# GFNet mixing and hard-swish MLP on one core: the filter step of batches two to eight with real and imaginary part side by side in columns

## The chip, the cores and the metric

The kernel runs on one core of a Trainium2 chip. The metric is the device time of one execution in microseconds (us). One execution was also recorded by the hardware profiler; its page and its trace are what is read here. Engines are named as the profile names them: PE (TensorE, the matmuls), PEld (its weight loads), DVE (VectorE), ACT (ScalarE), POOL (GpSimd), SP (SyncE, which issues most DMAs).

## The reference

Two blocks in a row, all in float32. The first is a global filter: a real Fourier transform over the sequence, a product with a complex filter per frequency and channel, and the inverse transform. The second is an MLP with hard-swish on every token.

```python
batch, seq, dim = (8, 3008, 256)          # n_freq = 1505
X = np.fft.rfft(x, axis=1)
Y = X * (filt_r + 1j * filt_i)[None, :, :]
y = np.fft.irfft(Y, n=seq, axis=1)

h = y.reshape(24064, 256) @ w_in          # d_ff = 2048
g = h * np.clip(h + 3.0, 0.0, 6.0) / 6.0
out = g @ w_out
```

## The kernel before

The transform of length 3008 = 47 x 64 is done in two stages of matmuls with tables of cosines and sines, and the way back likewise. Per batch (numbered 0 to 7 in the code, one to eight here) the stages are: `a_unit` or `a6_unit` (sums over 47, results stored to `z_tmp` in HBM), `t2_load` (reads them back with k, part and column over the partitions), `b_unit` (sums over 64: the spectrum of two rows of k, in a PSUM bank), `f_unit` (products with the filter), `y_unit` (their sums: the filtered spectrum `y`), `bi3_unit` (first stage of the way back for three `y`, copied to a tile `t3`), `g3_store` (to `g_tmp` in HBM), `t4_load` and `n_five` or `n_unit` (second stage, giving `xn`, the token columns of the MLP). k runs over 24 values, four to a filter table, so a batch has six tables and twelve `f_unit`s.

The MLP works on 47 blocks of 512 tokens, each in 8 steps of 256 hidden columns. A step multiplies with Strassen-like sums: `up_1` to `up_5` make seven products with `w_in` in the PSUM tiles `al` and `be`, `hswish`, `g_sums` and `g_last` form the operands on DVE, `down` makes seven products with `w_out` in the four `po` banks. All matmuls go through `strips` (line 768), two column halves of 64 at a time. A step without other work takes 6.1 us.

The spectral stages of the next batch are put into these steps by hand: `at(step, fn, ...)` places a function at a step, `places(n)` holds the steps of `f_unit`, `y_unit` and `bi3_unit`, and the loop at the end writes the instruction streams in that order. Every engine works its stream in order. For batches three to eight (`n` 2 to 7), with k the first step of the batch's own tokens, `a6_unit` of the last chunk is at step k-41, `t2_load` and `table_load` of tables 0 and 1 at the end of step k-40, the first `b_unit` and `f_unit` in step k-38. In that step DVE runs `g_sums`, then `f_unit`, then `up_2b` (line 797, h from `be`) and the sum of `up_3` (line 802, h from `al`). TensorE's last `up` product, `up_5`, writes into `al` again, so it comes after line 802.

Real and imaginary part lie on the two halves of the partitions. `b_unit` (line 539) fills a bank with the real part on partitions 0 to 63 and the imaginary part on 64 to 127, two k in the columns. `f_unit` multiplies the whole bank with the filter (line 559), and for the crossed products each half with the other half of the filter (lines 563, 564). `y_unit` subtracts or adds halves (lines 573, 574), on 64 partitions each.

`table_load` (lines 259, 261) puts the filter in a table of 128 partitions: frequencies k + 47 q on the even rows of a quarter and the mirrored ones on the odd rows, hence a partition stride of two. For batches two to eight it issues 8 DMAs of 64 KB on SP's queue; there are two buffers (`FB = 2`), so table c waits for the last `f_unit` of table c-2. SP also issues `x_load`, `t2_load`, `t4_load` and all stores of the result, in program order.

Of the kernel before, what the change touches and what calls it, by code (L numbers as in the profile page):

```python
# [10 lines left out]
FP32 = mybir.dt.float32  # L11
I32 = mybir.dt.int32
AXT = mybir.ActivationFunctionType
# [14 lines left out]
NA = 47  # L28
# [50 lines left out]
def _make_tables():  # L79
# [12 lines left out]
    for k in range(KH):  # L92
        at = k // 4 * 4 + (0, 2, 1, 3)[k % 4]
        for j in range(HC):
            tw = 2 * np.pi * (((np.arange(2 * NA) * HC + j) * k) % N) / N
            to = 1 + j * ATOM + at % 2 * KH + at // 2
            w0[X0:X0 + 2 * NA, to], w0[X0:X0 + 2 * NA, to + NU] = np.cos(tw), -np.sin(tw)
    wi = np.zeros((P, 3, NC))
    wf = np.zeros((P, 4, 64))
    at_of = [q % 2 * 32 + q // 2 * 2 if q < 32 else (31 - q) % 2 * 32 + (q - 32) // 2 * 2 + 1 for q in range(64)]  # L100
    for q in range(64):
        g, sign = (q, 1.0) if q < 32 else (31 - q, -1.0)
        co, si = (f([2 * np.pi * ((j * g) % NC) / NC for j in range(HC + 1)]) for f in (np.cos, np.sin))
        ab = np.concatenate([co, np.zeros(HC - 1) if q == 63 else si[1:HC]])
        cd, dc = ab * np.where(np.arange(NC) > HC, -1.0, 1.0), np.roll(ab, HC)
        at = at_of[q]
        wi[at, 0], wi[HALF + at, 0] = cd, sign * dc
        cs, sn = (np.array([f(2 * np.pi * ((j * g) % NC) / NC) for j in range(HC)]) for f in (np.cos, np.sin))
        if g % 32 == 0:
            sn = np.zeros(HC)  # L110
        for r in range(0, P, HALF):
            wf[r:r + 32, g % 2, at % 32], wf[r + 32:r + 64, g % 2, at % 32] = cs, sn
            wf[r:r + 32, g % 2, 32 + at % 32], wf[r + 32:r + 64, g % 2, 32 + at % 32] = -sign * sn, sign * cs

        for h in range(2):
            s = -1.0 if h and g % 2 else 1.0
            wf[h:HALF:2, 2, at], wf[HALF + h::2, 2, at] = s * cs, s * sn
            wf[h:HALF:2, 3, at], wf[HALF + h::2, 3, at] = -s * sign * sn, s * sign * cs
        wi[at, 1], wi[HALF + at, 1] = cd, -cd
        wi[at, 2], wi[HALF + at, 2] = sign * dc, sign * dc  # L120
    start = np.eye(P)
# [45 lines left out]
                    direct[HALF + at_of[q], k - KH + TC, n * TOK:(n + 1) * TOK] = -2 / N * first_of(np.sin(th), n)  # L167
    wai = np.concatenate([t.reshape(P, -1) for t in (groups, ones, first, last)], axis=1)
    f = np.float32
    return wa.astype(f), w0.astype(f), wai.astype(f), wi.astype(f), wf.astype(f), start.astype(f), direct.astype(f)  # L170


@with_exitstack
def kernel(
# [8 lines left out]
):  # L183
    nc = tc.nc

    wa_np, w0_np, wai_np, wi_np, wf_np, start_np, direct_np = _make_tables()
    wa_d = nc.inline_tensor(wa_np, name="wa_t").ap()
    w0_d = nc.inline_tensor(w0_np, name="w0_t").ap()
    wai_d = nc.inline_tensor(wai_np, name="wai_t").ap()
    wi_d = nc.inline_tensor(wi_np, name="wi_t").ap()  # L190
    wf_d = nc.inline_tensor(wf_np, name="wf_t").ap()
    start_d = nc.inline_tensor(start_np, name="start_t").ap()
    direct_d = nc.inline_tensor(direct_np, name="direct_t").ap()
# [32 lines left out]
    edge = wai[:, ds(2 * (NJ + 1) * NA, ND)]  # L226
    edges = edge.rearrange("p (j n) -> p j n", n=TOK)
    wi = const.tile([P, 3, NC], FP32, name="wi")
    xs = const.tile([P, 3, XC, D], FP32, name="xs")
    ft_all = const.tile([P, FB * TC, D], FP32, name="ft")  # L230
    ft = [ft_all[:, ts(i, TC), :] for i in range(FB)]
# [10 lines left out]
    def raw(src, row, ap):  # L242
        return bass.AP(tensor=src.tensor, offset=src.offset + row * D, ap=ap)


    def table_load(b, c):
        n = TC if b else 2 * TC
        if n == TC:
            t = ft[(b * NT + c) % FB]
            st["ft", b, c] = t  # L250
        else:
            t = x0_at(HC * D - TC * D * c, 2 * TC * D).rearrange("p (k d) -> p k d", k=n) if c else ft_all
            for i in range(2):
                st["ft", b, c + i] = t[:, ts(i, TC), :]
        for src, p0 in ((filt_r, 0), (filt_i, HALF)):
            q = nc.gpsimd if p0 and b == 0 and c else nc.sync
            for r in range(2):
                o = p0 + 32 * r
                q.dma_start(t[o:o + 32:2, :, :].rearrange("p k d -> p (k d)"),
                                  raw(src, c * TC + NA * r, [[2 * NA * D, 16], [1, n * D]]))  # L260
                q.dma_start(t[o + 1:o + 32:2, :, :],
                                  raw(src, NA * (2 - r) - c * TC, [[2 * NA * D, 16], [-D, n], [1, D]]))
# [125 lines left out]
    def x0_at(o, n):  # L388
        return w_all.rearrange("p a b c m -> p (a b c m)")[:, ds(NP * 14 * P - HC * D + o, n)]
# [141 lines left out]
    def b_unit(b, i):  # L531
        c, r = divmod(2 * i, TC)
        if b != 1:
            t = st.pop(("t2", b, c))
            ps = [bank(b) for k in range(2)]
            for s_ in range(2):
                for ri in range(2):
                    for k in range(2):
                        nc.tensor.matmul(ps[k][ds(ri * 64 + s_ * 32, 32)].rearrange("p (v d) -> p v d", v=2),  # L539
                                         wf[ts(k, 64), s_, ts(ri, 32)], t[ts(k, 64), :, s_, :], start=True, stop=True)  # L540
            for k in range(2):
                st["ps", b, i + k] = ps[k].rearrange("p (u d) -> p u d", u=2)
            return
        ps = bank(b).rearrange("p (u d) -> p u d", u=2)
        for u in range(2):

            strips(ps[:, u, :], wf[:, 2:4, :].rearrange("p a m -> p (a m)"), st["t2", b, c][:, r // 2 + 2 * u, :], start=True, stop=True)
        st["ps", b, i] = ps

    def f_unit(b, i):  # L550
        c, r = divmod(2 * i, TC)
        ps = st.pop(("ps", b, i))
        f = st["ft", b, c][:, r:r + 2, :]

        pool_, n1, n2 = (hp, "h0", "h1") if b == 0 and i & 2 else (sp, "s1", "s2")
        s1, s2 = (pool_.tile([P, 512], FP32, name=n).rearrange("p (u d) -> p u d", u=2) for n in (n1, n2))

        re, im = slice(0, HALF), slice(HALF, P)
        nc.vector.tensor_tensor(out=s1, in0=ps, in1=f, op=ALU.mult)
        if ("tf", b, c) in st:  # L560
            nc.vector.tensor_tensor(out=s2, in0=ps, in1=st["tf", b, c][:, r:r + 2, :], op=ALU.mult)
        else:
            nc.vector.tensor_tensor(out=s2[re], in0=ps[re], in1=f[im], op=ALU.mult)
            nc.vector.tensor_tensor(out=s2[im], in0=ps[im], in1=f[re], op=ALU.mult)
        st["y", b, i] = s1, s2

    def y_unit(b, i):
        s1, s2 = st["y", b, i]
        if b == 0 and i % 2 == 0:
            st["y0"] = t1p.tile([P, 2, 2, D], FP32, name="t1")  # L570
        y = yp.tile([P, 2, D], FP32, name="y") if b else st["y0"][:, i % 2, :, :]
        re, im = slice(0, HALF), slice(HALF, P)
        nc.vector.tensor_tensor(out=y[re], in0=s1[re], in1=s1[im], op=ALU.subtract)
        nc.vector.tensor_tensor(out=y[im], in0=s2[re], in1=s2[im], op=ALU.add)
        st["y", b, i] = y
# [15 lines left out]
    def bi3_unit(b, i):  # L591
        ys = [st.pop(("y", b, i + v)) for v in range(3)]
        c = psU.tile([P, 512], FP32, name="be")
        banks = [psF.tile([P, 512], FP32, name="psf", tag="f") for ri in range(2)]
        t = t3p.tile([P, 3, 2, D], FP32, name="t3")
        to = [t[:, q, :, :].rearrange("p u d -> p (u d)") for q in range(3)]
        for r in range(3):
            for v in range(2):
                for ri in range(2):
                    x, u, ps, o = (2, v, c, ri) if r == 2 * ri else (v, r - 1 + ri, banks[ri], r - 1 + ri)  # L600
                    nc.tensor.matmul(ps[ts(v, 64), ts(o, D)], wi[ts(ri, 64), 0, :], ys[x][ts(ri, 64), u, :], start=True, stop=True)  # L601
            if r == 0:
                nc.vector.tensor_copy(out=to[2][:, 0:2], in_=c[:, 0:2])
        nc.scalar.activation(out=to[1], in_=banks[1], func=AXT.Copy)
        st["t3", b, i] = t
        st["bi3"] = to[0], banks[0], to[2], c

    def bi3_copies():
        if "bi3" in st:
# [3 lines left out]

    def g3_store(b, i):
        t = st.pop(("t3", b, i))
        for v in range(2):
            nc.gpsimd.dma_start(g_d[b, :, :, ds(2 * (i + v), 2), :].rearrange("c ri u d -> c ri (u d)"),
                                t[ts(v, 64), 0:2].rearrange("p ri u d -> p ri (u d)"))
        for u in range(2):
            nc.gpsimd.dma_start(g_d[b, :, :, 2 * (i + 2) + u, :], t[ts(u, 64), 2])  # L620

    def g0_first(i):
        t = st["t3", 0, i]
# [142 lines left out]
    def strips(ps, w, x, **kw):  # L766
        for o in range(0, P, STRIP):
            nc.tensor.matmul(ps[ds(o, STRIP)], w[:, ds(o, STRIP)], x, skip_group_check=True, **kw)  # L768
# [214 lines left out]
    with tc.manual_schedule():  # L983
# [111 lines left out]
        def wai_load():  # L1095
            nc.sync.dma_start(wa[:, 528:], wa_d[:, 528:])
            nc.sync.dma_start(wai, wai_d[:, 0:NW])


        half = 0  # L1100
# [222 lines left out]
```

## Time and profile before

| | |
|---|---|
| median of 3 runs | 2602.68 us (2601.38 to 2606.01) |
| the profiled execution | 2602.51 us |
| its span in the profile | 2600.7 us |
| granted TensorE clock | 1.0 |
| DMA queue of SP (q1) | 114141 packets, 148.25 MB |
| filter loads of batches two to eight | 336 DMAs of 64 KB |

The page gives busy time and its share of the span for each engine, the chain of work that ended last, and groups of equal instructions: line, engine, operation, tiles written and read, shapes, count, then busy time, mean duration of one in ns, and the engine's idle time before them with what ended it. The timeline gives start (us from the span's start), duration, engine, line, operation and count, and in brackets the idle time before. A float32 matmul appears as two records, one for each pass.

### The profile page before, as it was taken

What the parts mean: (1) busy time and instruction counts of PE and PEld (TensorE: products, weight loads), DVE (VectorE), ACT (ScalarE), POOL (GpSimd) and SP (SyncE); (2) the same over time, 40 slices, a digit from 0 to 9 for tenths busy, and PEclk for the clock granted to TensorE, in tenths of its full rate; (3) what the DMA queues carried; (4) which work ended last, traced back from release to release, by engine and by line L of the source; (5) the groups of instructions that cost most, each with busy time, mean ns of one, the idle gap of its engine ahead of it and who ended that gap; (6) DMA issues with size and microseconds to landing.
All of it is one profiled execution on the core that took longest, in us unless ns stands there. A gap on an engine that the chain in (4) does not pass through costs nothing.

```text
span 2600.7 us, 87032 instructions
## 1 busy us (share of the span) xinstructions
PE 2584.9 (99%) x37890; PEld 2049.8 (79%) x37890; DVE 2026.2 (78%) x3610; ACT 1298.2 (50%) x2682; POOL 481.6 (19%) x721
## 2 busy tenths in 40 slices
PE   8999999999999999999999999999999999999999
PEld 4487777888778887788877887778877888888887
DVE  6978877887778877788777887788877888766666
ACT  4554454545544455454454544545545454455554
POOL 3252021111211112111131111311113111111110
PEclk9999999999999999999999999999999999999999
DMA  8733234213341123411233212332223421110000
GB/s 235 219 94 85 56 103 117 54 40 81 80 118 54 43 78 83 115 54 43 78 92 106 56 51 68 91 106 59 56 63 89 106 62 46 50 45 24 20 22 26
DMA packets 129843, 199.25 MB, mean 77 GB/s; under 512 B 21570, under 2 KB 97312, under 8 KB 129078
## 3 DMA queue, kind: packets, MB, share of 16 engines
q1 hardware_dynamic: 114141, 148.25, 21.1%
q0 software_dynamic: 15040, 45.21, 6.4%
q8 instruction: 297, 4.87, 0.8%
q14 instruction: 84, 0.69, 0.1%
q10 hardware_dynamic: 281, 0.24, 0.0%
HBM read 121.35 MB, written 83.98 MB: 79 GB/s over the span
## 4 chain that ended last, share of the span: by engine, by line
PE 97%; DVE 1%; DMA 1%; issue 0%; ACT 0%; SPq 0%; POOL 0%; POOLq 0%; DVEq 0%; ACTq 0%
PE po L768 45%; PE al L768 25%; PE be L768 19%; PE psf L539 1%; PE psf L480 1%; PE psn L708 1%; PE al L708 1%; PE psf L601 1%; PE be L601 1%; PE be L480 1%; DMA g_tmp<-t 0%; PE psf L768 0%; PE psf L453 0%; PE psn L768 0%; DVE g L821 0%
## 5 line engine op out<-in xcount | busy, mean ns | idle before, releaser
L768 PEld LDWEIGHTS po<-w_all,g 128*64 128x64 f32 x20808 | 1239.1, 137 | 248.5 <-issue 12.8
L768 PE MATMUL po<-w_all,g 128*64 128x128 f32 (+1 forms) x20808 | 1409.8, 274 | 1.5 <-DVE g L821 0.9
L816 ACT ACTIVATE r<-h,half_c 128x512 f32<-128x512 f32 x736 | 531.0, 721 | 322.5 <-DVE h L797 310.5
L768 PE MATMUL al<-xt,w_all 128*64 128x256 f32 x4416 | 665.3, 379 | 0.1
L821 DVE SCALAR_TENSOR_TENSOR g<-r,h 128x512 f32<-128x512 f32 x736 | 529.3, 719 | 167.0 <-ACT r L816 153.2
L768 PE MATMUL be<-xt,w_all 128*64 128x256 f32 x2944 | 443.5, 379 | 0.0
L797 DVE TENSOR_TENSOR h<-be,s 128x512 f32<-128x512 f32 x368 | 253.8, 690 | 108.8 <-PE be L768 88.5
L768 PEld LDWEIGHTS be<-xt,w_all 128*64 128x64 f32 x2944 | 212.4, 137 | 105.5
L811 ACT ACTIVATE h<-al 128x256 f32<-128x256 f32 x368 | 141.4, 384 | 286.2 <-PE al L768 285.5
L768 PEld LDWEIGHTS al<-xt,w_all 128*64 128x64 f32 x4416 | 280.2, 137 | 1.2 <-POOL w_all L357 1.0
L802 DVE TENSOR_TENSOR h<-al,s 128x256 f32<-128x256 f32 x368 | 156.2, 424 | 149.5 <-PE al L768 145.2
L829 DVE TENSOR_TENSOR g<-g 128x512 f32<-128x512 f32 x367 | 254.8, 694 | 12.6
L768 PE MATMUL al<-xn,w_all 128*64 128x256 f32 (+1 forms) x1536 | 240.5, 393 | 1.0 <-DVE g L821 0.6
L792 ACT ACTIVATE s<-al 128x256 f32<-128x256 f32 x368 | 141.5, 385 | 191.9 <-PE al L768 191.8
L768 PE MATMUL be<-xn,w_all 128*64 128x256 f32 (+1 forms) x1536 | 236.9, 388 | 0.0
L783 ACT ACTIVATE s<-be 128x256 f32<-128x256 f32 x368 | 141.4, 384 | 172.2 <-PE be L768 172.2
L763 POOL TENSOR_TENSOR xt<-xn 128x256 f32<-128x256 f32 x184 | 144.1, 825 | 358.9 <-ACT xn L688 358.9
L782 ACT ACTIVATE s<-al 128x256 f32<-128x256 f32 x368 | 141.5, 385 | 78.8 <-PE al L768 78.8
L925 POOL TENSOR_TENSOR o<-p,o 128x256 f32<-128x256 f32 x46 | 36.4, 790 | 771.6 <-DVE o L923 689.1
L828 DVE TENSOR_TENSOR g<-g 128x256 f32<-128x256 f32 x367 | 158.6, 432 | 12.6
L834 DVE TENSOR_TENSOR g<-g 128x256 f32<-128x256 f32 x367 | 157.3, 429 | 3.2
L768 PEld LDWEIGHTS be<-xn,w_all 128*64 128x64 f32 x1536 | 111.1, 137 | 61.7 <-issue 7.4
(170 smaller groups left out, 1858.3 us busy)
## 6 DMA issues: line engine op xcount, KB each, us to landing
t<-g_tmp SPq DMA_DIRECT2D x184, 120.0 KB
t<-z_tmp SPq DMA_DIRECT2D x42, 512.0 KB
g_tmp<-t POOLq DMA_DIRECT2D x68, 256.0 KB, 4.2
z_tmp<-t POOLq DMA_DIRECT2D x120, 144.0 KB, 3.4
o_tmp<-o SPq DMA_DIRECT2D x46, 256.0 KB
xs<-in_x_dram SPq DMA_DIRECT2D x60, 192.0 KB
ft<-in_filt_r_dram SPq DMA_DIRECT2D x168, 64.0 KB
ft<-in_filt_i_dram SPq DMA_DIRECT2D x168, 64.0 KB
```

What stands on the lines that cost most here:

```text
L763: nc.gpsimd.tensor_tensor(out=o, in0=x0, in1=x1, op=op_)
L768: nc.tensor.matmul(ps[ds(o, STRIP)], w[:, ds(o, STRIP)], x, skip_group_check=True, **kw)
L782: nc.scalar.activation(out=s[:, 0, :], in_=al, func=AXT.Copy)
L783: nc.scalar.activation(out=s5, in_=be[:, 1, :], func=AXT.Copy)
L792: nc.scalar.activation(out=s[:, 1, :], in_=al, func=AXT.Copy)
L797: nc.vector.tensor_tensor(out=st["h"][0].rearrange("p (a n) -> p a n", a=2), in0=be, in1=s, op=ALU.add)
L802: nc.vector.tensor_tensor(out=st["h"][1][:, 256:512], in0=al, in1=s5, op=ALU.add)
L816: nc.scalar.activation(out=r, in_=st["h"][i], func=AXT.Relu, bias=half_c, scale=1.0 / 6.0)
L821: nc.vector.scalar_tensor_tensor(out=st["g", k, p][:, o:o + 2, :].rearrange("p a n -> p (a n)"), in0=st["r", i], scalar=1.0, in1=st["h"][i ...
L828: v.tensor_tensor(out=g[:, G1, :], in0=g[:, G3, :], in1=g[:, G22, :], op=ALU.add)
L829: v.tensor_tensor(out=g[:, G3:G2 + 1:2, :], in0=g[:, G3:G1 + 1, :], in1=g[:, G11:G11 + 1, :].broadcast_to([P, 2, 256]), op=ALU.subtract)
L834: nc.vector.tensor_tensor(out=g[:, G4, :], in0=g[:, G12, :], in1=g[:, G2, :], op=ALU.subtract)
```

## The change

For batches two to eight the bank, the filter table and `y` are turned: two k lie over the two halves of the partitions, real and imaginary part side by side in the columns. Batch one keeps its layout.

- `b_unit` of batches three to eight issues 16 matmuls of 256 columns where it had 8 of 512. Batch two keeps four matmuls of 256 columns.
- `f_unit` has two operations of 128x512, the second with the filter's two parts in reversed order (`f[:, ::-1]`); `y_unit` two of 128x256.
- `bi3_unit` takes its weights from a new table `wi2` (64 KB, loaded with the other tables in the opening) and swaps the roles of rows and columns; counts and shapes of its matmuls stay.
- the tile `t3` then holds six rows of k in a row for each partition, and `g3_store` writes it with two DMAs instead of four.
- `table_load` issues 16 DMAs of 32 KB for a table instead of 8 of 64 KB.

```diff
     def table_load(b, c):
-        n = TC if b else 2 * TC
-        if n == TC:
-            t = ft[(b * NT + c) % FB]
-            st["ft", b, c] = t
...
+        if b:
+            t = st["ft", b, c] = ft[(b * NT + c) % FB].rearrange("p (ri k) d -> p ri k d", ri=2)
+            for ri, src in enumerate((filt_r, filt_i)):
+                for v in range(2):
+                    for r in range(2):
+                        o = v * HALF + 32 * r
+                        nc.sync.dma_start(t[o:o + 32:2, ri], raw(src, c * TC + v + NA * r, [[2 * NA * D, 16], [2 * D, 2], [1, D]]))
+                        nc.sync.dma_start(t[o + 1:o + 32:2, ri], raw(src, NA * (2 - r) - c * TC - v, [[2 * NA * D, 16], [-2 * D, 2], [1, D]]))
+            return
...
+            else:
                 for ri in range(2):
-                    for k in range(2):
-                        nc.tensor.matmul(ps[k][ds(ri * 64 + s_ * 32, 32)].rearrange("p (v d) -> p v d", v=2),
-                                         wf[ts(k, 64), s_, ts(ri, 32)], t[ts(k, 64), :, s_, :], start=True, stop=True)
+                    for s_ in range(2):
+                        for v in range(2):
+                            for k in range(2):
+                                nc.tensor.matmul(ps[k][ds(v * 64 + s_ * 32, 32), ts(ri, D)], wf[ts(k, 64), s_, ts(ri, 32)],
+                                                 t[ts(k, 64), v, s_, :], start=True, stop=True)
...
     def f_unit(b, i):
         c, r = divmod(2 * i, TC)
         ps = st.pop(("ps", b, i))
+        if b:
+            s1, s2 = (sp.tile([P, 512], FP32, name=n).rearrange("p (u d) -> p u d", u=2) for n in ("s1", "s2"))
+            f = st["ft", b, c][:, :, r // 2, :]
+            nc.vector.tensor_tensor(out=s1, in0=ps, in1=f, op=ALU.mult)
+            nc.vector.tensor_tensor(out=s2, in0=ps, in1=f[:, ::-1], op=ALU.mult)
+            st["y", b, i] = s1, s2
+            return
...
     def y_unit(b, i):
         s1, s2 = st["y", b, i]
-        if b == 0 and i % 2 == 0:
+        if b:
+            y = yp.tile([P, 2, D], FP32, name="y")
+            nc.vector.tensor_tensor(out=y[:, 0, :], in0=s1[:, 0, :], in1=s1[:, 1, :], op=ALU.subtract)
+            nc.vector.tensor_tensor(out=y[:, 1, :], in0=s2[:, 0, :], in1=s2[:, 1, :], op=ALU.add)
+            st["y", b, i] = y
+            return
...
         for r in range(3):
-            for v in range(2):
-                for ri in range(2):
-                    x, u, ps, o = (2, v, c, ri) if r == 2 * ri else (v, r - 1 + ri, banks[ri], r - 1 + ri)
-                    nc.tensor.matmul(ps[ts(v, 64), ts(o, D)], wi[ts(ri, 64), 0, :], ys[x][ts(ri, 64), u, :], start=True, stop=True)
+            for ri in range(2):
+                for v in range(2):
+                    x, ps, o = (2, c, v) if r == 2 * v else (r - 1 + v, banks[v], r - 1 + v)
+                    nc.tensor.matmul(ps[ts(ri, 64), ts(o, D)], wi2[ts(v, 64), ri, :], ys[x][ts(v, 64), ri, :], start=True, stop=True)
...
     def g3_store(b, i):
         t = st.pop(("t3", b, i))
-        for v in range(2):
-            nc.gpsimd.dma_start(g_d[b, :, :, ds(2 * (i + v), 2), :].rearrange("c ri u d -> c ri (u d)"),
-                                t[ts(v, 64), 0:2].rearrange("p ri u d -> p ri (u d)"))
-        for u in range(2):
-            nc.gpsimd.dma_start(g_d[b, :, :, 2 * (i + 2) + u, :], t[ts(u, 64), 2])
+        for ri in range(2):
+            nc.gpsimd.dma_start(g_d[b, :, ri, ds(2 * i, 6), :].rearrange("c k d -> c (k d)"),
+                                t[ts(ri, 64)].rearrange("p x v d -> p (x v d)"))
...
             nc.sync.dma_start(wai, wai_d[:, 0:NW])
+            nc.sync.dma_start(wi2, wi2_d)
```

More of the change, by code (lines that the diff above doesn't have):

```diff
@@ L98, in _make_tables @@
     wi = np.zeros((P, 3, NC))
+    wi2 = np.zeros((P, 2, NC))
     wf = np.zeros((P, 4, 64))
@@ L118, in _make_tables @@
             wf[h:HALF:2, 3, at], wf[HALF + h::2, 3, at] = -s * sign * sn, s * sign * cs
+        for r in range(0, P, HALF):
+            wi2[r + at, 0], wi2[r + at, 1] = cd, sign * dc
         wi[at, 1], wi[HALF + at, 1] = cd, -cd
@@ L169, in _make_tables @@
     f = np.float32
-    return wa.astype(f), w0.astype(f), wai.astype(f), wi.astype(f), wf.astype(f), start.astype(f), direct.astype(f)
+    return tuple(t.astype(f) for t in (wa, w0, wai, wi, wi2, wf, start, direct))
 @with_exitstack
@@ L184 @@
     nc = tc.nc
-    wa_np, w0_np, wai_np, wi_np, wf_np, start_np, direct_np = _make_tables()
+    wa_np, w0_np, wai_np, wi_np, wi2_np, wf_np, start_np, direct_np = _make_tables()
     wa_d = nc.inline_tensor(wa_np, name="wa_t").ap()
@@ L190 @@
     wi_d = nc.inline_tensor(wi_np, name="wi_t").ap()
+    wi2_d = nc.inline_tensor(wi2_np, name="wi2_t").ap()
     wf_d = nc.inline_tensor(wf_np, name="wf_t").ap()
@@ L228 @@
     wi = const.tile([P, 3, NC], FP32, name="wi")
+    wi2 = const.tile([P, 2, NC], FP32, name="wi2")
     xs = const.tile([P, 3, XC, D], FP32, name="xs")
@@ L246, in table_load @@
     def table_load(b, c):
-        n = TC if b else 2 * TC
-        if n == TC:
-            t = ft[(b * NT + c) % FB]
-            st["ft", b, c] = t
[L251 to L254, printed above, removed]
+        if b:
[7 more added lines that the diff above has]
+            return
+        n = 2 * TC
+        t = x0_at(HC * D - TC * D * c, 2 * TC * D).rearrange("p (k d) -> p k d", k=n) if c else ft_all
+        for i in range(2):
+            st["ft", b, c + i] = t[:, ts(i, TC), :]
         for src, p0 in ((filt_r, 0), (filt_i, HALF)):
@@ L535, in b_unit @@
             ps = [bank(b) for k in range(2)]
-            for s_ in range(2):
-                for ri in range(2):
-                    for k in range(2):
-                        nc.tensor.matmul(ps[k][ds(ri * 64 + s_ * 32, 32)].rearrange("p (v d) -> p v d", v=2),
-                                         wf[ts(k, 64), s_, ts(ri, 32)], t[ts(k, 64), :, s_, :], start=True, stop=True)
+            if b == 0:
+                for s_ in range(2):
+                    for ri in range(2):
+                        for k in range(2):
+                            nc.tensor.matmul(ps[k][ds(ri * 64 + s_ * 32, 32)].rearrange("p (v d) -> p v d", v=2),
+                                             wf[ts(k, 64), s_, ts(ri, 32)], t[ts(k, 64), :, s_, :], start=True, stop=True)
+            else:
+                for ri in range(2):
+                    for s_ in range(2):
+                        for v in range(2):
+                            for k in range(2):
+                                nc.tensor.matmul(ps[k][ds(v * 64 + s_ * 32, 32), ts(ri, D)], wf[ts(k, 64), s_, ts(ri, 32)],
+                                                 t[ts(k, 64), v, s_, :], start=True, stop=True)
             for k in range(2):
@@ L544, in b_unit @@
         ps = bank(b).rearrange("p (u d) -> p u d", u=2)
-        for u in range(2):
-            strips(ps[:, u, :], wf[:, 2:4, :].rearrange("p a m -> p (a m)"), st["t2", b, c][:, r // 2 + 2 * u, :], start=True, stop=True)
+        for ri in range(2):
+            for v in range(2):
+                nc.tensor.matmul(ps[ts(v, 64), ri, :], wf[:, 2 + ri, :], st["t2", b, c][:, r // 2 + 2 * v, :],
+                                 start=True, stop=True, skip_group_check=True)
         st["ps", b, i] = ps
@@ L552, in f_unit @@
         ps = st.pop(("ps", b, i))
+        if b:
[5 more added lines that the diff above has]
+            return
         f = st["ft", b, c][:, r:r + 2, :]
-        pool_, n1, n2 = (hp, "h0", "h1") if b == 0 and i & 2 else (sp, "s1", "s2")
+        pool_, n1, n2 = (hp, "h0", "h1") if i & 2 else (sp, "s1", "s2")
         s1, s2 = (pool_.tile([P, 512], FP32, name=n).rearrange("p (u d) -> p u d", u=2) for n in (n1, n2))
@@ L568, in y_unit @@
         s1, s2 = st["y", b, i]
-        if b == 0 and i % 2 == 0:
+        if b:
[4 more added lines that the diff above has]
+            return
+        if i % 2 == 0:
             st["y0"] = t1p.tile([P, 2, 2, D], FP32, name="t1")
-        y = yp.tile([P, 2, D], FP32, name="y") if b else st["y0"][:, i % 2, :, :]
+        y = st["y0"][:, i % 2, :, :]
         re, im = slice(0, HALF), slice(HALF, P)
@@ L595, in bi3_unit @@
         t = t3p.tile([P, 3, 2, D], FP32, name="t3")
-        to = [t[:, q, :, :].rearrange("p u d -> p (u d)") for q in range(3)]
         for r in range(3):
-            for v in range(2):
-                for ri in range(2):
-                    x, u, ps, o = (2, v, c, ri) if r == 2 * ri else (v, r - 1 + ri, banks[ri], r - 1 + ri)
-                    nc.tensor.matmul(ps[ts(v, 64), ts(o, D)], wi[ts(ri, 64), 0, :], ys[x][ts(ri, 64), u, :], start=True, stop=True)
+            for ri in range(2):
+                for v in range(2):
+                    x, ps, o = (2, c, v) if r == 2 * v else (r - 1 + v, banks[v], r - 1 + v)
+                    nc.tensor.matmul(ps[ts(ri, 64), ts(o, D)], wi2[ts(v, 64), ri, :], ys[x][ts(v, 64), ri, :], start=True, stop=True)
             if r == 0:
-                nc.vector.tensor_copy(out=to[2][:, 0:2], in_=c[:, 0:2])
-        nc.scalar.activation(out=to[1], in_=banks[1], func=AXT.Copy)
+                nc.vector.tensor_copy(out=t[:, 2, 0, 0:2], in_=c[:, 0:2])
+        two = [ps.rearrange("p (x d) -> p x d", x=2) for ps in banks]
+        nc.scalar.activation(out=t[:, 0:2, 1, :], in_=two[1], func=AXT.Copy)
         st["t3", b, i] = t
-        st["bi3"] = to[0], banks[0], to[2], c
+        st["bi3"] = t[:, 0:2, 0, :], two[0], t[:, 2, :, :].rearrange("p v d -> p (v d)"), c
     def bi3_copies():
@@ L615, in g3_store @@
         t = st.pop(("t3", b, i))
-        for v in range(2):
-            nc.gpsimd.dma_start(g_d[b, :, :, ds(2 * (i + v), 2), :].rearrange("c ri u d -> c ri (u d)"),
-                                t[ts(v, 64), 0:2].rearrange("p ri u d -> p ri (u d)"))
-        for u in range(2):
-            nc.gpsimd.dma_start(g_d[b, :, :, 2 * (i + 2) + u, :], t[ts(u, 64), 2])
+        for ri in range(2):
+            nc.gpsimd.dma_start(g_d[b, :, ri, ds(2 * i, 6), :].rearrange("c k d -> c (k d)"),
+                                t[ts(ri, 64)].rearrange("p x v d -> p (x v d)"))
     def g0_first(i):
```

## The prediction

> **What bounds the kernel now.** I read the page from the top: the span, the engines' busy time, then the chain that ended last.
>
> ```profile
> span 2600.7 us, 87032 instructions
> ...
> PE 2584.9 (99%) x37890; PEld 2049.8 (79%) x37890; DVE 2026.2 (78%) x3610; ACT 1298.2 (50%) x2682; POOL 481.6 (19%) x721
> ...
> PE 97%; DVE 1%; DMA 1%; issue 0%; ACT 0%; SPq 0%; POOL 0%; POOLq 0%; DVEq 0%; ACTq 0%
> ```
>
> TensorE is without work for 2600.7 - 2584.9 = 15.8 us of the whole span, most of that in the opening. VectorE is at 78% and has 1% of the chain. So work taken from VectorE is worth next to nothing by itself, and anything that makes TensorE wait is paid in full. The next view, the groups of instructions with shapes kept apart, has what the change edits:
>
> ```profile
> L564 DVE TENSOR_TENSOR s<-psf,ft 64x512 f32<-64x512 f32 x84 | 58.4, 695 | 1.2
> L574 DVE TENSOR_TENSOR y<-s 64x512 f32<-64x512 f32 x84 | 58.3, 694 | 2.9
> L573 DVE TENSOR_TENSOR y<-s 64x512 f32<-64x512 f32 x84 | 58.1, 692 | 2.6
> L559 DVE TENSOR_TENSOR s<-psf,ft 128x512 f32<-128x512 f32 x84 | 57.5, 684 | 3.2 <-PE psf L539 2.9 <-DMA out_dram<-o 0.2
> L563 DVE TENSOR_TENSOR s<-psf,ft 64x512 f32<-64x512 f32 x84 | 57.4, 683 | 1.2
> ...
> L539 PE MATMUL psf<-t,wf 64*32 64x512 f32 x576 | 40.0, 601 | 0.0
> ```
>
> An operation on 64 partitions (683 to 695 ns) costs what one on 128 does (684 ns). The free size sets the price.
>
> **Part 1, VectorE.** `f_unit`: three operations become two of 128x512: 84 x 0.69 = 58 us less. `y_unit`: two of 64x512 become two of 128x256; the nearest rows, 128x256 sums within SBUF, take 425 to 432 ns, so 84 x 2 x (0.693 - 0.43) = 44 us less. VectorE falls by about 102 us. On the path I put this at nothing: 35 of the 36 `b_unit`s of batches 3 to 8 need the same 1.02 us from their first matmul to the next product (one needs 1.79), so hardly a late VectorE result shows there. VectorE's side could give at most what PE's weight loads waited for it in these steps (rival 2).
>
> **Part 2, TensorE.** A `b_unit` now has 8 matmuls of 512 columns (16 records, two passes each) and will have 16 of 256 (32 records). In the timeline of PE:
>
> ```profile
> 1202.83 0.60 PE L768 MATMUL be<-xt,w_all 128*64 128x256 f32 x4
> 1203.36 1.09 PE L539 MATMUL psf<-t,wf 64*32 64x512 f32 x16
> 1204.38 0.66 PE L768 MATMUL po<-w_all,g 128*64 128x128 f32 x8
> ```
>
> Eight tiles run side by side: two passes of 0.427 us each, plus 0.17 us of loading and of changing the tile shape. Afterwards four passes of half the length follow each other. `bi3_unit` (line 601) already runs passes of 256 columns on four tiles, and there they start every 0.216 us, against 0.213 us of pure streaming, with the weight loads inside. So +0.01 to +0.03 us each, 36 x 0.02 = 0.7 us. The upper bound is the dearest small matmul in the trace, `n_five`: 80 records of 47 columns in 1.31 us, 16.4 ns each; 16 more records at that price would be 0.26 us, x 36 = 9.4 us. I take 0.7, because 256 columns are the shape of line 601. `bi3_unit` keeps its count and shapes, batch 2's `b_unit` its 4 matmuls. ACT copies the same 512 columns.
>
> The Trainium skill, page "TensorEngine Tiling (Array Packing)", section "Performance Considerations", speaks against the split: it gives each matmul some 60 cycles of overhead on trn2. At 0.42 ns a cycle that is an estimate of 25 ns for each of 16 more passes, 14 us in all if they added up; the passes of line 601 start 3 ns beyond pure streaming, so this trace does not show that overhead where tiles overlap.
>
> **Part 3, the stores.** `g3_store` issues two DMAs instead of four: 56 fewer on POOL's queue, at 0.6 to 0.69 us (lines 617, 620). POOL is 19% busy and off the chain: nothing. `wi2` is one more load of 64 KB on SP in the opening, 0.4 us ahead of `t4` loads whose matmuls come 13 us after the last of them: nothing.
>
> **Part 4, the filter loads on SP.** Here the cover is thin. A table (4 rows of k, real and imaginary) was 8 DMAs of 64 KB and becomes 16 of 32 KB, 336 issues more. What does one cost? In the timeline of SP, at batch 5's first table:
>
> ```profile
> 1062.01 0.58 SPq L259 DMA_DIRECT2D ft<-in_filt_r_dram  x1
> 1062.63 0.61 SPq L261 DMA_DIRECT2D ft<-in_filt_r_dram  x1
> ...
> 1066.48 0.60 SPq L261 DMA_DIRECT2D ft<-in_filt_i_dram  x1
> 1067.13 0.60 SPq L525 DMA_DIRECT2D t<-z_tmp  x1
> 1067.77 0.55 SPq L259 DMA_DIRECT2D ft<-in_filt_r_dram  x1
> 1068.36 2.54 SPq L261 DMA_DIRECT2D ft<-in_filt_r_dram  x1
> ```
>
> They follow each other every 0.64 us, whether a DMA has 16 runs of 4 KB (line 259) or 64 of 1 KB (line 261). The new ones have 32 runs of 1 KB with the same stride over partitions, so I take 0.64; the cheapest two-dimensional load on SP (`xs`, 0.33 us, partitions in one run) is the other end. A table then needs 10.2 us of issues instead of 5.1.
>
> Table 0 of batches 3 to 8 has the least room. `places` loads it at the end of step k-40, behind `t2_load`, which waits for the spectrum; `f_unit` uses it in step k-38. VectorE in that step:
>
> ```profile
> 1071.00 0.69 DVE L559 TENSOR_TENSOR s<-psf,ft 128x512 f32<-128x512 f32 x1 [0.20 <-PE psf L539]
> 1071.71 0.68 DVE L563 TENSOR_TENSOR s<-psf,ft 64x512 f32<-64x512 f32 x1
> 1072.40 0.69 DVE L564 TENSOR_TENSOR s<-psf,ft 64x512 f32<-64x512 f32 x1
> 1074.56 0.69 DVE L797 TENSOR_TENSOR h<-be,s 128x512 f32<-128x512 f32 x1 [1.47 <-PE be L768]
> 1075.17 0.41 DVE L802 TENSOR_TENSOR h<-al,s 128x256 f32<-128x256 f32 x1
> ```
>
> Count from the table's first issue. The last of 16 issues ends at +10.2; a filter load's semaphore is complete 1.7 us after its issue ends (1.6 to 1.8 where nothing disturbs it); some 0.15 us for VectorE's waits on eight DMA semaphores: `f_unit` can start at +12.0 instead of about +8.9, and its two operations end at +13.4. Queued behind it on VectorE is line 797 (h from `be`), then line 802, which frees `al` for `up_5`. Before, line 797 started at +11.96, +11.66, +12.55, +11.95, +12.45 and +12.13 in batches 3 to 8, and TensorE's `al` product came 0.1 to 0.2 us after 802 ended. So TensorE is held by 1.2, 1.5, 0.7, 1.2, 0.75 and 1.1 us: 6.5 us together. The two shorter operations of part 1 are in this; at the old `f_unit` it would be 0.7 more each.
>
> Some issues take longer: 2.54 us above, 0.94 to 1.8 us elsewhere; nearly all such begin within 0.9 us of a 16 KB packet of the instruction queue. Over the 42 tables these pauses add up to 25 us, 0.6 us for each 5.1 us of issues. Now table 0 spans 10.2 us and a pause anywhere in it goes to the end: 1.2 us on average, but the first half of these loads had almost none before. I take 0.8, six times: 5 us; bounds 0 and 2 each.
>
> The other tables have room: table 1 of batches 3 to 8 ends some 27 us before its first use, the later ones 38 to 64; batch 2's table 0 ends 8.0 us before (needed: 5.1 + 1.85), its table 1 15.3 (needed: 10.2 + 1.85), the later ones 16 or more. `t2_load` of tables 1 and 2 and the `t4` loads behind come up to 12 us later, with 15 us left or more.
>
> **Sum.** 6.5 + 5 + 0.7 = 12.2 us on the profiled execution's 2602.51 us (span and 1.8 us around it; the median of the runs is 2602.68): 2614.7 us.
>
> **Rivals.**
> 1. *The loads stay hidden* (0.22). If an issue of 32 KB costs 0.50 us, the 16 take 8.0 us and line 797 could start at +11.2, before its old place; only pauses are left. For it: no row has this shape, and contiguous partitions cost 0.33. Against it: 16 and 64 runs at that stride cost the same. Time: 2602.5 + 0.7 + about 1 = 2604.
> 2. *Faster: VectorE's relief reaches TensorE* (0.04). The waits list PE's weight loads after L829 for 10.1 us, L828 for 10.1 and L834 for 4.5, all in steps with `b_unit` or `bi3_unit`. Results that come earlier by 0.5 to 0.7 us could end those waits, 24.7 us at most; a half gives 2590. It decides if over a fifth of those 24.7 us stopped the matmuls. Against it: 15.8 us of idle PE in all, and 1.02 us 35 times in 36.
> 3. *The short matmuls cost more* (0.08): 9.4 us by `n_five`'s price; alone 2612, with the table wait 2624.
> 4. *The forecast*, a wait for table 0 (0.66): 2605 to 2626.
>
> **Numbers.** This kernel's measurement can tell about 0.2%, 5.2 us. Slower by more: nine tenths of case 4 (0.60), rival 3 (0.08) and some of rival 1 (0.02) make 0.70; within: the rest of 4 and most of 1, 0.25; faster: rival 2 and a bit of 1, 0.05. The range goes from 2602 (most of rival 1, case 4 without pauses) to 2628 (two us of pauses in each batch, or rival 3 on top).
>
> **What would show it.** In the profile after: filter loads at 0.64 us each on SP; `f_unit`'s first operation in six places with a wait for a DMA of `ft`; a gap of 1 to 3 us on PE ahead of `al` in the same step, and nowhere else; VectorE some 102 us less busy; 1.02 to 1.05 us per `b_unit`. I am wrong if the issues cost half as much, if the gaps are absent, or if the time comes out below 2597.

## The result and the profile after

| | before | after |
|---|---|---|
| median | 2604.40 us (2601.38 to 2606.16, 6 runs) | 2618.31 us (2614.55 to 2619.61, 6 runs) |
| profiled execution | 2602.51 us | 2618.61 us |
| its span | 2600.7 us | 2616.5 us |
| granted TensorE clock, mean | 1.0 | 0.997 |
| packets on SP's queue (q1) | 114141 | 127725 |
| DMAs issued by GpSimd | 278 | 222 |

The ratio of the times is 1.0052, 95% interval 1.0039 to 1.0065: slower, by half a per cent. The profile page of the changed kernel, with its span, the busy time of each engine and the shares of the chain that ended last:

```profile
span 2616.5 us, 88296 instructions
...
PE 2588.6 (99%) x38466; PEld 2067.2 (79%) x38466; DVE 1892.7 (72%) x3526; ACT 1298.1 (50%) x2682; POOL 440.4 (17%) x665
...
PE 95%; DMA 2%; SPq 2%; DVE 1%; issue 0%; POOL 0%; ACT 0%; POOLq 0%; DVEq 0%
```

VectorE fell from 78% to 72% and the kernel lost time. In the chain DMAs and SP's issues now hold 2% each, where they had 1% and 0%. The groups of instructions with shapes kept apart show the two edited steps:

```profile
L575 DVE TENSOR_TENSOR s<-psf,ft 128x512 f32<-128x512 f32 x84 | 57.6, 686 | 28.5 <-DMA ft<-in_filt_i_dram 17.3 <-PE al L798 4.2 <-PE be L798 3.5
...
L557 PE MATMUL psf<-t,wf 64*32 64x256 f32 x1152 | 39.4, 382 | 0.0
```

Read the last column, VectorE's idle time ahead of the operation: ahead of `f_unit`'s first one it was 3.2 us before and is 28.5 now, most of it for a filter load. The last of these waits is for batch eight's table 0. The timeline of SP, from its first issue, its two long ones and its last:

```profile
2039.95 0.59 SPq L258 DMA_DIRECT2D ft<-in_filt_r_dram  x1
2040.59 0.59 SPq L259 DMA_DIRECT2D ft<-in_filt_r_dram  x1
...
2046.31 1.41 SPq L258 DMA_DIRECT2D ft<-in_filt_i_dram  x1
...
2050.31 1.47 SPq L259 DMA_DIRECT2D ft<-in_filt_i_dram  x1
```

Sixteen issues, each 0.64 us after the one ahead of it, and two pauses of 0.8 and 0.9 us: the last ends 11.83 us after the first began. What VectorE does with that is easiest to see in batch three (timeline of VectorE, then of TensorE; the bracket is the idle time before and what ended it):

```profile
425.39 0.69 DVE L575 TENSOR_TENSOR s<-psf,ft 128x512 f32<-128x512 f32 x1 [4.74 <-DMA ft<-in_filt_i_dram]
426.00 0.68 DVE L576 TENSOR_TENSOR s<-psf,ft 128x512 f32<-128x512 f32 x1
426.60 0.68 DVE L827 TENSOR_TENSOR h<-be,s 128x512 f32<-128x512 f32 x1
427.20 0.41 DVE L832 TENSOR_TENSOR h<-al,s 128x256 f32<-128x256 f32 x1
```

```profile
427.66 0.65 PE L798 MATMUL al<-xn,w_all 128*64 128x256 f32 x4 [1.98 <-DVE h L832]
428.15 1.09 PE L798 MATMUL po<-w_all,g 128*64 128x128 f32 x16
429.02 1.07 PE L798 MATMUL al<-xt,w_all 128*64 128x256 f32 x4
...
432.43 0.60 PE L798 MATMUL al<-xt,w_all 128*64 128x256 f32 x4
```

VectorE waits 4.74 us for the table, and the sums of lines 827 and 832 (797 and 802 before) queue behind it, so TensorE waits 1.98 us for `al`. Then comes something that the sum had no term for: from 429.02 to 432.4 us, four records of matmuls that take 0.60 us elsewhere take 1.07. The granted clock is 0.5 there.

To find where the time went I paired the MLP matmuls of both traces one by one and took the difference of their starts, the lag. It moves only at some places (times of before):

| place | lag gained, us |
|---|---|
| opening, up to 60 | -0.4 |
| batch two, five places from 172.9 to 308 | -2.6 |
| table 0 of batches three to eight (428.7, 752, 1075.6, 1399, 1723, 2046.7) | 3.88, 0.1, 0.88, 1.93, 1.59, 4.71: 13.1 |
| 1568, a stop that the kernel before has and this one has not (experiment 3) | -0.8 |
| 1785 and 1826 | 0.55 + 1.07 = 1.6 |
| last matmul | 10.84 (sum of the rows: 10.9) |
| behind the last matmul | 10.33 instead of 5.39: 4.9 |

10.84 + 4.93 = 15.8 us, the difference of the spans. So the late tables are the largest term, but there are three more of 1.6 to 4.9 us: a gain in batch two, a loss at 1785 and 1826 without a late table, and an end that is 4.9 us longer. The experiments take these apart.

### The profile page after: what moved, and what is told of

It is laid out like the page before. It is cut to its first block, busy times and chain, and to the rows that moved or that the text cites. A ratio compares the mean times of both kernels' runs of the same rounds, so it can differ in the third digit from the quotient of the medians.

```text
span 2616.5 us, 88296 instructions
## 1 busy us (share of the span) xinstructions
PE 2588.6 (99%) x38466; PEld 2067.2 (79%) x38466; DVE 1892.7 (72%) x3526; ACT 1298.1 (50%) x2682; POOL 440.4 (17%) x665
## 3 DMA queue, kind: packets, MB, share of 16 engines
q1 hardware_dynamic: 127725, 148.34, 21.0%
## 4 chain that ended last, share of the span: by engine, by line
PE 95%; DMA 2%; SPq 2%; DVE 1%; issue 0%; POOL 0%; ACT 0%; POOLq 0%; DVEq 0%
PE po L798 43%; PE al L798 25%; PE be L798 18%; PE psf L490 1%; PE psf L557 1%; PE psn L738 1%; PE psf L632 1%; SPq L258 1%; PE al L738 1%; PE be L632 1%; SPq L259 1%; PE be L490 1%; DMA z_tmp<-t 0%; DMA bits<-in_moe_w_in_dram 0%; PE psf L565 0%
## 5 line engine op out<-in xcount | busy, mean ns | idle before, releaser
L851 DVE SCALAR_TENSOR_TENSOR g<-r,h 128x512 f32<-128x512 f32 x736 | 523.9, 712 | 199.1 <-ACT r L846 195.8
```

The costliest lines, as they stand in the source:

```text
L851: nc.vector.scalar_tensor_tensor(out=st["g", k, p][:, o:o + 2, :].rearrange("p a n -> p (a n)"), in0=st["r", i], scalar=1.0, in1=st["h"][i ...
```

## The experiments

The theories: A, the sixteen issues make table 0 late; C, VectorE's relief is what gains in batch two; E, the longer end goes with GpSimd's DMAs; and, for what then is left, that the greater number of short matmuls costs TensorE something.

**1. The late table (A): table 0 asked for five steps earlier.** `early` is the changed kernel with

```diff
                 s = f_at[2 * (c - FB) + 1] + 1 if c >= FB else a_at[-1] + 1
+                if n > 1 and c == 0:
+                    s = a_at[-1] - 4
                 at(s, table_load, n, c)
```

> The changed kernel with table 0 of batches three to eight issued three steps earlier (step k-45 in place of k-40), nothing else. Theory A (the six waits for table 0, plus the clock drops that two of them set off, are the loss): f_unit waits for no filter DMA, no gap over 0.5 us on PE ahead of al in step k-38, no clock of 0.5 within the run; 9.7 us of gaps and 2.9 us of slow clock go away, so 2618.3 - 12.6 = 2605.7 us, with the long end of the program (4.9 us more than before) still in it, 2601 without. Rival B (the turned layout costs the time in the matmuls or on VectorE): stays within 3 us of 2618.

The edit moves the load by five steps, from k-40 to k-45; "three" is a slip.

Measured: 2606.66 us (2605.43 to 2610.63, 11 runs) beside 2602.85 of the kernel before on the same chip, ratio 1.0017 (1.0008 to 1.0025). The profiled execution took 2605.74 us, span 2603.8. The same group of its profile:

```profile
L575 DVE TENSOR_TENSOR s<-psf,ft 128x512 f32<-128x512 f32 x84 | 57.5, 685 | 5.9 <-PE psf L557 5.5 <-DMA out_dram<-o 0.4
```

`f_unit` waits for no filter load any more, the clock stays at 1 up to the last matmul, and that comes 1.90 us earlier than in the kernel before instead of 10.84 later. Of these 12.74 us the opening, which differs from execution to execution, has 0.95; on the other side `early` loses 2.6 us at 1717, 1785 and 1826 where the changed kernel loses 1.6, and gains 0.4 less at 1568. So the late table is worth 13.2 us, its slow clock included, against 13.1 read at the six places.

**2. The number of issues alone (A): the kernel before with each filter DMA cut in two.** `before16` leaves layout, matmuls and VectorE's work as they were:

```diff
-                q.dma_start(t[o:o + 32:2, :, :].rearrange("p k d -> p (k d)"),
-                                  raw(src, c * TC + NA * r, [[2 * NA * D, 16], [1, n * D]]))
+                for k0, m in ((0, 2), (2, 2)) if b else ((0, n),):
+                    q.dma_start(t[o:o + 32:2, k0:k0 + m, :].rearrange("p k d -> p (k d)"),
+                                raw(src, c * TC + k0 + NA * r, [[2 * NA * D, 16], [1, m * D]]))
```

and likewise for the mirrored rows.

> The kernel before, only each filter DMA of 64 KB of batches two to eight split into two of 32 KB (two rows of k each). Theory A: the number of issues alone makes the loss; table 0 is as late as after the change, and f_unit's three operations end 0.7 us later than two: gaps on PE of 0.8 to 3.8 us in each of batches three to eight, 14 us together, and 1.5 us of slow clock behind each gap of over 2 us: 2617 to 2624 us. Rival B: no change of layout, so no loss, 2603 +- 3 us.

Measured: 2611.9 us (2604.02 to 2616.8, 6 runs), ratio 1.0030 (1.0018 to 1.0043); profiled 2616.8, span 2615.0. Its waits (engine, what for, us in total, times, longest):

```profile
PE al L769 <- DVE h L803: 9.3, 5, 2.4
...
DVE s L560 <- DMA ft<-in_filt_i_dram: 8.6, 3, 3.8
```

The same wait at the same place, without anything else of the change: the six places gain 14.0 us of lag, 3.4 of it from two windows at half clock. A stands. But the runs of this kernel spread over 12.8 us, and the profiled one is the slowest of the six; the median lies below what I expected, and the fastest run (2604.02) lies among those of the kernel before, so a table of sixteen issues does not cost this much in every execution.

**3. VectorE's relief alone (C).** `light` is the kernel before with the changed kernel's operations on VectorE for batches two to eight (two products of 128x512, two sums of 128x256). The sums then pair the wrong halves, so the crossed products are not those of the reference.

```diff
+        if b:
+            nc.vector.tensor_tensor(out=s2, in0=ps, in1=f, op=ALU.mult)
...
+        if b:
+            nc.vector.tensor_tensor(out=y[:, 0, :], in0=s1[:, 0, :], in1=s1[:, 1, :], op=ALU.subtract)
+            nc.vector.tensor_tensor(out=y[:, 1, :], in0=s2[:, 0, :], in1=s2[:, 1, :], op=ALU.add)
```

> The kernel before with only VectorE's work of the changed one: f_unit makes two products of 128x512 with the same filter half (the crossed products are left out) and y_unit two sums of 128x256; loads, matmuls and stores as before. Theory C (VectorE's relief does reach TensorE): 2.4 us less in batch two and 0.8 us in the one late b_unit of batch six, about 2599.5 us. Rival D (TensorE was never late for VectorE there, the earlier places come from something else): 2602.7 +- 1 us.

Measured: 2599.95 us (2597.86 to 2601.15, 11 runs), ratio 0.9988 (0.9979 to 0.9996), profiled 2599.95. In batch two the lag moves by the same steps as in the changed kernel: -0.44, -0.34, -0.34, -0.53 and -0.95. One of them in the timeline of the weight loads, `light`:

```profile
305.32 0.85 PEld L774 LDWEIGHTS po<-w_all,g 128*64 128x64 f32 x16 [0.29 <-DVE o L930]
```

In the kernel before the same loads start at 307.90 with 0.78 us of waiting for the same VectorE sum. Relief of VectorE does reach TensorE, in batch two, by 2.6 us in these five steps.

The 0.8 us that I expected in batch six came too (-0.74 at 1568), but it is not VectorE's. In the kernel before, the weight loads of that `b_unit` stop, and no semaphore ends the stop:

```profile
1566.12 0.16 PEld L539 LDWEIGHTS psf<-t,wf 64*32 64x32 f32 x11
1566.92 0.15 PEld L539 LDWEIGHTS psf<-t,wf 64*32 64x32 f32 x5 [0.64 <-issue]
```

`light` has no such stop there, but one of 0.67 us at 1393.85, where its lag grows by 0.57. And `earlym` (experiment 6), with the same relief, has one of 0.91 us in the same `b_unit`. Experiment 8 comes back to these stops.

**4. The end (E): the stores written as four DMAs again.** `stores4` is the changed kernel with

```diff
         for ri in range(2):
-            nc.gpsimd.dma_start(g_d[b, :, ri, ds(2 * i, 6), :].rearrange("c k d -> c (k d)"),
-                                t[ts(ri, 64)].rearrange("p x v d -> p (x v d)"))
+            for x, m in ((0, 2), (2, 1)):
+                nc.gpsimd.dma_start(g_d[b, :, ri, ds(2 * (i + x), 2 * m), :].rearrange("c k d -> c (k d)"),
+                                    t[ts(ri, 64), x:x + m].rearrange("p x v d -> p (x v d)"))
```

> The changed kernel with g3_store as four DMAs again (per part: four rows of k, then two), so POOL's queue has as many instructions as before. Theory E (the end of the program, where POOL's last drain took 8.9 us in place of 3.6, hangs on POOL's shorter instruction stream): the end after the last matmul is back at 5.8 us, 2618.3 - 4.9 = 2613.4 us. Rival F (that end varies by itself or hangs on something else): 10.7 us after the last matmul, or now one and now the other; 2618 us in the median.

Measured: 2612.07 us (2609.43 to 2615.18, 5 runs), ratio 1.0036 (1.0024 to 1.0048). In the profiled execution (2609.61) 5.38 us lie behind the last matmul; GpSimd's last DRAIN takes 3.59 us, in the changed kernel 8.87. `f_unit` starts 12.7 to 14.4 us after table 0's first issue, about as in the changed kernel (12.7 to 14.3), yet the six places gain only 7.3 us of lag in this execution. So the end is priced by the trace (5.38 for 10.33 us) and not by the difference of the times alone.

**5. Both repairs together.** `early4` has the edits of 1 and 4.

> The changed kernel with table 0 of batches three to eight asked for five steps earlier and the six-row stores written as four DMAs. If the late table (12.8 us of TensorE lag) and the long end (4.9 us) are separate costs that add, the time is 2606.7 - 4.9 = 2601.8 us, from 0.5 to 2 us below the kernel before. If the stores' extra issues on GpSimd cost something that the shorter end hides, or if the long end only shows when TensorE is early, it stays near 2606.

Measured: 2601.92 us (2600.6 to 2602.47, 11 runs) beside 2603.07, ratio 0.9993 (0.9984 to 1.0002). The two costs add as expected, and in the profiled execution 5.27 us lie behind the last matmul. This is the fastest kernel here that does all the work of the reference, but the interval holds 1, so it isn't shown to beat the kernel before.

**6. What the end goes with.** Two kernels with table 0 early: `early3` writes each store as three DMAs, `earlym` as two, with three small memsets of GpSimd behind them.

```diff
+        for m in range(3):
+            nc.gpsimd.memset(pad, 0.0)
```

> The changed kernel with table 0 earlier and each six-row store as three DMAs, 28 more than in the changed kernel and 28 fewer than before. If the last DRAIN of GpSimd grows steadily with the missing DMAs, it takes about 6.2 us; if it is either short or long, by where GpSimd's stream ends, it takes 3.6 or 8.9 us.

> The changed kernel with table 0 earlier, two DMAs for each six-row store, and three one-column memsets on GpSimd behind each store: 84 instructions more on GpSimd, as many as the kernel before has, and no DMA more. If the long last DRAIN of GpSimd goes with the number of its instructions, it takes 3.6 us and the span is about 2599; if it goes with the number of DMAs that GpSimd issues, it takes 8.9 us and the span stays at 2603.8.

Measured, in one execution each: `early3` 2605.25 us, 6.65 us behind the last matmul; `earlym` 2609.97 us, 10.32 us. The memsets bring GpSimd's instructions back to 1063, the number before, and the end stays long. So the count of instructions in the profile is not it. With 278, 250 and 222 DMAs the end is 5.3, 6.6 and 10.3 us. That is no steady growth, and not short or long either. In `early3` the chain of waits has a part that no other shows; its last rows, beside those of the changed kernel (start, us, engine or reason, tile or line):

```profile
2597.01 0.53 POOL out_dram L1003
2597.54 2.89 issue
2600.43 0.54 POOLq L1352
```

```profile
2606.36 0.51 POOL out_dram L1002
2606.87 0.53 POOLq L1349
```

In `early3` GpSimd stops for 2.89 us ahead of its last DMA and its closing instructions, and then drains for 2.26 us. What it drains, and why fewer DMAs make that longer, stays open; the last section has what goes with it. `earlym` is 4.4 us above my longer guess for the span (2608.2): its opening took 4.0 us longer than that of `early`, 1.7 of it with half a clock.

**7. Gaps made on purpose.** `ladder` is the kernel before with 2 to 7 more products on VectorE ahead of the first `f_unit` of batches three to eight; no DMA is changed.

```diff
+        for m in range(b if b > 1 and i == 0 else 0):
+            nc.vector.tensor_tensor(out=s1, in0=ps, in1=f, op=ALU.mult)
         nc.vector.tensor_tensor(out=s1, in0=ps, in1=f, op=ALU.mult)
```

> The kernel before with b products more (128x512, 0.69 us each) on VectorE ahead of the first product of batch three (b = 2) to eight (b = 7), so that the first strips wait for VectorE longer and longer, with no DMA changed. The six gaps should be about 0.69 b - 1.3: 0.1, 0.8, 1.5, 2.1, 2.8 and 3.5 us. If the granted clock falls after a gap of some length, as it did after gaps of 2.15 and 3.08 us and not after 1.93, it falls to 0.5 for 3.4 us after the last three and each of these costs 1.3 to 1.7 us beyond its gap: lag 10.8 from gaps and 4.5 from the clock, span about 2616. If the fall belonged to the late transfers and not to the gap, the clock stays at 1 and the span is about 2611.5.

The gaps of the changed kernel that stand here as 2.15, 3.08 and 1.93 us are 1.98, 2.81 and 1.76 in the brackets of its trace.

Measured, in one execution: 2616.09 us, span 2614.0. The lag steps are 0, 0.71, 1.44, 3.89, 2.89 and 3.64 us: 0.69 us per product, as expected, with 1.8 more in the fourth alone. So a slow clock follows a gap that has nothing to do with DMAs, but my rule for it was wrong: it came after the gap of 1.99 us and not after those that cost 2.89 and 3.64. In the timeline of TensorE, the fourth and the sixth:

```profile
1404.24 0.98 PE L770 MATMUL al<-xn,w_all 128*64 128x256 f32 x4 [1.99 <-DVE h L804]
...
2060.14 0.65 PE L770 MATMUL al<-xn,w_all 128*64 128x256 f32 x4 [2.22 <-DVE h L804]
```

0.98 us at half clock in the first, 0.65 at full clock in the second, behind the longer gap. `before16` has the same pair, a drop after a gap of 1.97 us and none after 2.43. What tells them apart is in the last section.

**8. Short matmuls alone.** `short` is the kernel before with each `b_unit` matmul of 512 columns written as two of 256, in the old layout (batches three to eight; batch two has short ones already).

```diff
-                    for k in range(2):
+                    for v in range(2) if b else ():
+                        for k in range(2):
+                            nc.tensor.matmul(ps[k][ds(ri * 64 + s_ * 32, 32), ts(v, D)],
+                                             wf[ts(k, 64), s_, ts(ri, 32)], t[ts(k, 64), v, s_, :], start=True, stop=True)
+                    for k in () if b else range(2):
                         nc.tensor.matmul(ps[k][ds(ri * 64 + s_ * 32, 32)].rearrange("p (v d) -> p v d", v=2),
                                          wf[ts(k, 64), s_, ts(ri, 32)], t[ts(k, 64), :, s_, :], start=True, stop=True)
```

> The kernel before with b_unit of batches two to eight in the changed kernel's number of matmuls: each of 512 columns written as two of 256, in the old layout, everything else as before. If two short matmuls cost TensorE no more than one long one, b_unit stays at 1.02 us, and the time is within 0.5 us of the kernel before. The changed kernel with table 0 early still lost 0.3 to 1.4 us at each of three or four places (at 1242, 1717, 1785 and 1826 us of the kernel before), with a pause that ends in nothing the profile names. If that comes from TensorE's longer stream of instructions, the same pauses are here and the time is about 2.5 us longer, 2605.5; if it comes from the transfers or the new order of the stores, they are not here and the time is 2603 to 2603.5. If short matmuls cost 0.1 to 0.5 us a step more, it is 6 to 16 us longer.

Measured: 2608.22 us (2605.34 to 2611.76, 11 runs) beside 2603.28, ratio 1.0018 (1.0008 to 1.0027). The pauses are here: the lag gains 0.65, 0.50, 1.72, 0.62 and 0.56 us at 1242, 1566, 1717, 1785 and 1826, 4.05 us together, and 1.5 us in small steps elsewhere, as a `b_unit` without a pause takes 1.064 us here instead of 1.019; that is more than the 2.5 I expected. The longest, in the timeline of the weight loads:

```profile
1720.88 0.63 PEld L540 LDWEIGHTS psf<-t,wf 64*32 64x32 f32 x28
1723.07 0.14 PEld L540 LDWEIGHTS psf<-t,wf 64*32 64x32 f32 x4 [1.56 <-issue]
```

28 of 32 loads, a stop of 1.56 us that no semaphore ends, then the last four. The three stops over 0.6 us in `short` end 2.7 to 2.8 us after a 16 KB packet of the instruction queue starts, those in `early` and `early4` 2.4 to 2.6 us after one. They come where `n_five`, whose records start every 16 ns, and `b_unit` follow each other, which is where TensorE uses up instructions fastest. That it waits for instructions fits all of this. It is argued: no run changed the fetching itself. That more pauses come with the longer stream of matmuls, and not with the transfers or the stores, is shown by this run. They are not new with it: the stop of 0.64 us in the kernel before (experiment 3) ends 2.6 us after such a packet, that of 0.67 us in `light` 2.8.

The Trainium skill, page "Runtime: NRT & Kernel Launch", section "Instruction fetch mechanics", says that instructions come in blocks of 16 KiB and that crossing a block costs little, "mostly hidden". The packets here have that size, and most are hidden; five stops of 0.5 to 1.7 us in this run are not.

## Why the prediction was right, point by point

The forecast was 2614.7 us by a wait for table 0 in batches three to eight; measured were 2618.61 in the profiled execution and 2618.31 in the median. The mechanism was right. The sum of 12.2 against 16.1 us (2618.61 - 2602.51) is short by 3.9, and it is closer than its terms.

- **Part 4, the price of an issue.** 0.64 us was right, also for the new shape, and rival 1 (0.50 us, loads hidden) falls with it. The last of 16 issues ended 10.6 to 12.4 us after the first: pauses of 0.5 to 2.2 us where I took 0.8, together 8.2 us where I took 5.
- **Part 4, the hold on TensorE.** 11.5 us were forecast, 13.1 came, but not as I had it. (The six terms of the working go with an end of `f_unit` at +13.2, not the +13.4 written there; its operations follow each other every 0.61 us, so +13.2 fits.) Without the slow clock the six lags sum to some 9.7 us (13.1 less 2 x 1.7). In batch four I expected 1.5 us and a pause and there was 0.1: SP's loads began 2.0 us earlier relative to TensorE than before, and in batches five and six 1.2 to 1.5 us earlier. I had taken the start as fixed. The half clock, 3.4 us that no term of mine had, more than put back the 1.8 us by which the gaps fell short, so the agreement is partly luck.
- **Part 3, the stores.** "Nothing" was wrong by 4.9 us, the worst term. I looked at GpSimd's queue, which is off the path until the last store of the kernel; the end behind it (5.4 us, in the profile before too) I had not examined.
- **Part 1 and rival 2, VectorE.** The rows gave 102 us less; by the sum of durations it is 110, by the page's busy time 133.5. On the path I put it at nothing for want of late results in batches three to eight. That holds there: the one `b_unit` of 1.79 us was late by a stop of TensorE's own (experiment 3). But in batch two relief gave -2.6 us (the whole of `light` by its ratio: -3.1), so it was no zero. It did not come through the lines that rival 2 lists: the weight loads' waits for 828, 829 and 834 fell from 24.7 to 14.2 us in the changed kernel, and no step of the lag lies at them. At the five steps the weight loads waited for lines 821 and 924. Rival 2 did not decide.
- **Part 2 and rival 3, the short matmuls.** A `b_unit` takes 1.024 us to the next product instead of 1.019: 0.005 each, below even the lower end. The cost sits elsewhere: 1.6 us (2.5 in `early4`, 4.1 in `short`) in pauses of TensorE, less the 0.8 us of the one that the kernel before has at 1568. This term had no place in the sum. The 14 us that the prediction estimates from the 60 cycles of the Trainium skill, page "TensorEngine Tiling (Array Packing)", section "Performance Considerations", are not there.
- **What would show it.** The waits for `ft` and the 0.64 us came as described, and the gaps ahead of `al` in five of the six places, with 0.7 to 2.8 us; "nowhere else" was wrong by the tail and the two pauses.

So the errors are +4.9 (end), +0.8 (pauses) and +3.4 (clock) against -2.6 (relief), -0.4 (opening), -1.8 (gaps, 9.7 for 11.5) and -0.5 (`b_unit`): 9.1 us one way and 5.3 the other. That the sum is off by only 3.9 is luck in part.

## What to carry to other kernels

When a layout is turned to make an engine's operations wider, count what the new layout does to the DMAs that fill it: here 110 us of work off an engine that hardly bounds cost some 13 us, because a transfer took twice the issues. A load that only fits because of its issue count should be asked for earlier in the same edit; with that and the old stores the change is level with the kernel before. And the end of a kernel is part of the path of every engine, also of one that is idle 80% of the time.

## What the runs showed of the hardware

**The clock is granted by fixed windows.** In every trace all changes of the granted clock lie a whole number of times 3.4133 us apart. In the changed kernel they come at 429.01, 432.42, 2057.17 and 2060.58 us: 2057.17 - 429.01 = 1628.16 = 477 x 3.4133. So I cut the traces on that grid. Busy time in such windows (us; then busy time and, in brackets, instructions of PE, PEld, DVE, ACT and POOL, then the granted clock, DMA share and GB/s), in the changed kernel:

```profile
425.60:429.01 3.41, 1.43 (x22) 1.21 (x22) 3.03 (x6) 1.34 (x3) 0.48 (x1) 1.00 0.55 182
429.01:432.42 3.41, 3.41 (x24) 2.29 (x22) 2.23 (x4) 1.26 (x3) 0.00 (x0) 0.50 0.20 52
1726.08:1729.49 3.41, 1.99 (x30) 1.53 (x28) 2.66 (x6) 1.71 (x3) 0.67 (x1) 1.00 0.45 145
```

in `before16`:

```profile
755.02:758.43 3.41, 1.90 (x26) 1.62 (x28) 2.48 (x6) 1.83 (x3) 0.00 (x0) 1.00 0.37 115
...
1406.96:1410.38 3.42, 1.45 (x24) 1.06 (x22) 3.23 (x7) 0.72 (x1) 1.24 (x2) 1.00 0.58 193
1410.38:1413.79 3.41, 3.41 (x28) 2.68 (x26) 2.53 (x5) 1.49 (x3) 0.00 (x0) 0.50 0.19 49
```

and in `ladder`:

```profile
1401.02:1404.43 3.41, 1.42 (x22) 1.10 (x20) 3.33 (x6) 0.54 (x1) 1.57 (x3) 1.00 0.59 184
...
2056.38:2059.79 3.41, 1.54 (x25) 1.30 (x19) 3.32 (x6) 0.00 (x1) 0.73 (x1) 1.00 0.53 185
```

The first figure after the comma, TensorE's busy time, tells the two kinds apart. Behind windows with 1.04 to 1.45 us of busy TensorE the clock was 0.5 for the next window (six of them, in four kernels); behind those with 1.54 to 1.99 us it stayed at 1. The gap of 2.43 us in `before16` lies across a border, 0.9 us in one window and 1.5 in the next; that of 1.97 lies within one. That is why the length of a gap does not tell. The price is 3.41 us at half speed, 1.7 us of TensorE's work. In the opening, with other shapes, the border was not as clean: a window with 1.74 us was followed by a drop in `earlym`, one with 1.66 was not in `early3`. Nor is it at the end: the last window with work in `early4` has 1.43 us (2593.99 to 2597.40), and the clock stayed at 1 through the empty one behind it. So that busy time alone decides is not shown.

The Trainium skill, page "TensorE: Matmul & The Clock Gate", section "What's actually happening", gives a free-running window of 3413 ns, which these traces show to the third digit. Its table lets the clock fall after at least one idle window; here it fell after windows in which TensorE was busy for 1.04 to 1.45 of 3.41 us, behind gaps as short as 1.97 us.

**GpSimd's last DRAIN goes with how the stores are split.** It took 3.6 to 3.7 us in the seven kernels with 278 DMAs issued by GpSimd and 8.9 in the three with 222, and 84 memsets more change nothing. One thing goes with it in all eleven traces: when the packets of 8 KB come that the page lists as instruction queue q14. Where the DRAIN is short, the last of them starts 0.8 us or 16.7 to 16.8 us ahead of it. Where it is long, the last starts 43 to 59 us ahead, and the next one 2.5 us after the DRAIN has ended. In `early3` one starts 0.9 us ahead of the stop of 2.89 us. That points at the fetching of instructions here too, but no run changed it, and the cause stays open.
